# Storing turned attention features by bands of 32 partitions, with the turn two and the store four steps later

## The chip, the cores and the metric

One core of a Trainium2 chip runs the kernel. The metric is the time of one execution on the device in microseconds (us). The engines are named as in the profile: PE is TensorE (matmul) and PEld its weight load, DVE is VectorE, ACT is ScalarE, POOL is GpSimd, and SP (SyncE) issues the DMAs.

## The reference

```python
xn = layernorm(x)                                   # x: 1 x 2048 x 1024
q, k, v = split(xn @ wqkv)                          # 32 heads of 32
pq, pk = q @ w_phi[h], k @ w_phi[h]                 # per head
phi(p) = concat(softmax(p), softmax(-p))            # 64 features a head
num = phi(pq) @ (phi(pk).T @ v)
den = phi(pq) . sum(phi(pk)) + 1e-6
s = (num / den) @ wo
g = silu((sigmoid(xn @ w_gate) * (xn @ w_up)) @ w_down)      # w_gate, w_up: 1024 x 3584
out = x + s * g
```

All of it is in fp32.

## The kernel before, in words

Each large product is done as seven products of blocks in place of eight (B11, B21, T2, T3, T4, T1, B22, in this order), with sums of blocks ahead of and behind them. A number is split into a high and a low part: ACT casts the high part (L137), DVE subtracts it to get the low one (L138), and `mm3` (L146 to L148) makes three matmuls of each pair. PE therefore runs the whole program through, and all else is fitted beside it.

The change lies in the down-projection (`w_down`). It goes through the products, 14 blocks of the inner dimension each, in two halves of four banks; B22 goes through its 14 blocks once for each half. A half of a step is 4 banks x 3 matmuls = 12 matmuls, and then one tick of a counter. `down_load` loads a block of weights (L926) and of activations (L928) into raw buffers (`fa`, `fb`), `down_prep` splits them (L137, L138) into `x` and `w` operands. At the end of a product each bank goes through `evacuate`: behind B21, DVE copies the bank out (L1810), ACT fills it again with the sum kept from B11 (L1811), and the next product, T2, adds to it; behind T1, DVE adds the bank to a kept sum (L1820). `gate_out` applies the gate: ACT (L1794), POOL (L1795), and a store (L1796).

Beside it the query features are finished, in 32 units: 16 tiles of 128 tokens by 2 halves of the heads. Unit n is queued by `q_late` at tick 2 + 24n/5. `later(n, f)` puts a function on the tick n ahead; `tick()` emits what stands on the present tick, behind the latest instruction that was emitted on DVE, ACT and SP. A list scheduler then sets the order of each engine, so ticks order instructions, but nothing on the chip waits for a tick. The steps of a unit are: load of exponentials or raw queries; for raw ones, minimum and maximum (L664, L665), differences (L673, L674), exponentials (ACT, L686) and their sums (L691, L692); `weigh`, a product on POOL in two instructions (L1005); `density`, a row sum and four small ones on DVE (L1010 to L1016); `scale`, a product on POOL in two (L1022); `turn`, a transpose on DVE of 128x1024 by blocks of 32 by 32 (L1026) into one of four slots (`etr`, slots 20 to 23); and `keep`, four stores from that slot to `et_d` in DRAM (L1030).

Behind the last unit, during product B22, the first attention work starts. It loads turned features (L1057), casts them on ACT (L1070) and subtracts on DVE (L1072). The first output of L1070 is slot 20, which was one of the four slots of turned features: it waits for the last turn and for the last stores. In the instruction order below, `x_3_9793` is the block with the four slots of turned features, and `x_4_15940` is what L1070 writes, in the same memory.

The DMAs of SP take turns on eight completion counters (DMAHW0 to DMAHW7 in the order): a DMA is issued only once the one eight places ahead of it has landed. SP issues in order, so a DMA that waits holds up all behind it.

The functions that the diff touches, and what calls them:

Of the kernel before, what the change touches and what calls it, by code (L numbers as in the profile page):

```python
# [19 lines left out]
S, D, H, DH, F = 2048, 1024, 32, 32, 3584  # L20
# [14 lines left out]
class Ring:  # L35
# [3 lines left out]
    def next(self):  # L39
        self.n += 1  # L40
        return self.items[(self.n - 1) % len(self.items)]
# [9 lines left out]
def hedgehog_glu_kernel(  # L51
# [12 lines left out]
    nc = tc.nc  # L64
# [16 lines left out]
    et_d = dram.tile([TT, 2, P, 2 * HB], F32, name="et_d")  # L81
# [39 lines left out]
    def whole(i):  # L121
        return slots[i].rearrange("p a n -> p (a n)")
# [33 lines left out]
    def later(n, f, *a):  # L156
        assert n > 0
        plan.setdefault(clock[0] + n, []).append((f, a))
# [500 lines left out]
    def extremes(name, p):  # L659

        nh = HB // DH
        st = small.tile([P, 4, nh], F32, name=f"st{name}", tag="st", bufs=2)
        pv = p.rearrange("p (h d) -> p h d", d=DH)
        nc.vector.tensor_reduce(st[:, 0], pv, axis=AX.X, op=ALU.max)  # L664
        nc.vector.tensor_reduce(st[:, 1], pv, axis=AX.X, op=ALU.min)  # L665
        return st

    def spread_q(st, p, e):

        pv, mx, mn = [a.rearrange("p (k b d) -> p k b d", b=2, d=d) for a, d in ((p, DH), (st[:, 0], 1), (st[:, 1], 1))]  # L670
        mx, mn = [a.to_broadcast([P, 8, 2, DH]) for a in (mx, mn)]
        ev = e.rearrange("p (b t k d) -> p t k b d", b=2, t=2, d=DH)
        nc.vector.tensor_tensor(ev[:, 0], pv, mx, op=ALU.subtract)  # L673
        nc.vector.tensor_tensor(ev[:, 1], mn, pv, op=ALU.subtract)  # L674
# [10 lines left out]
    def exponentials(e):  # L685
        nc.scalar.activation(e, e, AF.Exp)  # L686

    def inverses(st, e):

        s2, r2 = [st[:, a:a + 2].rearrange("p t h -> p (t h)") for a in (2, 0)]  # L690
        nc.vector.tensor_reduce(s2, e.rearrange("p (g d) -> p g d", d=DH), axis=AX.X, op=ALU.add)  # L691
        nc.vector.reciprocal(r2, s2)  # L692
        return r2
# [284 lines left out]
    def q_late(at, t, hb):  # L978

        hold = {}  # L980

        def load():
            if t < QA:
                hold["e"] = whole(eqr.next())
                nc.sync.dma_start(hold["e"], e_d[t, hb])
                hold["r"] = small.tile([P, 32], F32, name=f"r{t}{hb}", tag="r", bufs=2)
                nc.sync.dma_start(hold["r"], r_d[t, hb])
            else:
                hold["p"] = qraw.next()
                nc.sync.dma_start(hold["p"], qkv_d[Q, t, hb])  # L990

        def first():
            hold["st"] = extremes(f"q{t}{hb}", hold["p"])

        def second():
            hold["e"] = whole(eqr.next())
            spread_q(hold["st"], hold["p"], hold["e"])

        def sums():
            hold["r"] = inverses(hold["st"], hold["e"])  # L1000

        def weigh():
            for a in range(2):
                cols = slice(a * HB, (a + 1) * HB)
                nc.gpsimd.tensor_mul(whole(52)[:, cols], hold["e"][:, cols], zb[hb][:, cols])  # L1005

        def density():
            st = hold["sa"] = small.tile([P, 5, 16], F32, name=f"sa{t}{hb}", tag="sa", bufs=2)
            r, d2, r2 = hold["r"], *[st[:, a:a + 2].rearrange("p t h -> p (t h)") for a in (0, 2)]
            nc.vector.tensor_reduce(d2, whole(52).rearrange("p (g d) -> p g d", d=DH), axis=AX.X, op=ALU.add)  # L1010
            nc.vector.tensor_mul(d2, d2, r)
            r, d2, r2 = [a.rearrange("p (b t k) -> p b t k", b=2, t=2) for a in (r, d2, r2)]
            den = st[:, 4].rearrange("p (b k) -> p b k", b=2)
            nc.vector.scalar_tensor_tensor(den, d2[:, :, 0], EPS_DEN, d2[:, :, 1], op0=ALU.add, op1=ALU.add)
            nc.vector.reciprocal(den, den)
            nc.vector.tensor_mul(r2, r, den[:, :, None].to_broadcast([P, 2, 2, 8]))  # L1016

        def scale():
            e3, r2 = hold["e"].rearrange("p (g d) -> p g d", d=DH), hold["sa"][:, 2:4].rearrange("p t h -> p (t h)")
            for a in range(2):  # L1020
                gs = slice(16 * a, 16 * a + 16)
                nc.gpsimd.tensor_mul(e3[:, gs], e3[:, gs], r2[:, gs, None].to_broadcast([P, 16, DH]))  # L1022

        def turn():
            hold["et"] = whole(etr.next())
            nc.vector.transpose(hold["et"], hold["e"])  # L1026

        def keep():
            for c in range(4):
                nc.sync.dma_start(et_d[t, hb, c * DH:(c + 1) * DH].rearrange("f (a x) -> a f x", a=4),  # L1030
                                  hold["et"][:, c * 256:(c + 1) * 256])

        heavy = ((5, first), (6, second), (9, lambda: exponentials(hold["e"])), (11, sums))
        steps = ((0, load),) + heavy if t >= QA else ((6, load),)
        for n, f in steps + ((11, weigh), (14, density), (15, scale), (18, turn), (18, keep)):
            later(at + n, f)


# [157 lines left out]
    scale = {}  # L1196
# [154 lines left out]
    with in_order(*[getattr(mybir.EngineType, e) for e in ("PE", "DVE", "Activation", "SP", "Pool")]):  # L1351
        for name in FIRST:
            f, found = next((f, m) for form, f in forms for m in [re.fullmatch(form, name)] if m)
# [283 lines left out]
    for n, (kind, c, what, i) in enumerate(ops):  # L1637
# [48 lines left out]
        phase, f = c, what  # L1686
# [144 lines left out]
    for n in range(2 * TT):  # L1831
        q_late(2 + n * 24 // 5, *(light if (n + 1) * QA // TT > n * QA // TT else heavy).popleft())
# [225 lines left out]
```

## Time and profile before

| what | value |
|---|---|
| median of 3 runs | 2350.68 us (2350.02 to 2358.0) |
| time of the profiled execution | 2348.29 us |
| its span (first to last instruction) | 2346.5 us |
| mean granted PE clock | 0.943 of full speed |
| busy: PE, DVE, ACT, POOL | 2307.9, 1750.8, 1231.1, 1153.2 us |
| turns (L1026), 32 | 1634.2 to 2049.6 us |
| stores of turned features (L1030), 128 | 1635.4 to 2054.0 us |
| first attention cast (L1070) | 2062.05 us |

A row of the page or of a view names line, engine, operation and tiles (`out<-in`), how many there were, and the idle time of the engine ahead of them with what ended it. In a timeline the first two numbers are start and length in us, and the bracket holds that idle time.

### The profile page before, as it was taken

The numbers are of one execution on the slowest core, as the hardware profiler recorded it, in microseconds if no ns is written. First come the engines' busy times: TensorE is split into PE (matmuls) and PEld (weight loads), VectorE is DVE, ScalarE is ACT, GpSimd is POOL, SyncE is SP. The second block draws the span as 40 slices with busy tenths as digits, with TensorE's granted clock in tenths as the row PEclk, the third lists the DMA queues.
The fourth block names the chain that finished last, engine by engine and source line by source line (L and its number), as shares of the span: only waits on it lengthen the run. The fifth ranks groups of instructions, "written<-read, shape, count | busy, mean of one in ns | idle before, by whom it ended". The sixth has DMA issues, their size and how long they took to land.

```text
span 2346.5 us, 32121 instructions
## 1 busy us (share of the span) xinstructions
PE 2307.9 (98%) x10533; PEld 1918.4 (82%) x10533; DVE 1750.8 (75%) x2107; ACT 1231.1 (52%) x1965; POOL 1153.2 (49%) x813
## 2 busy tenths in 40 slices
PE   9999999999999999999999999999989999998988
PEld 8888888888888888888888888888878888877777
DVE  8625777876888774777874665657999999977887
ACT  7354577776555555555555545444444345354543
POOL 1323436772231054665653666764464445424676
PEclk9999999999999999999999999999989999989989
DMA  8789977988778868897886867679767666786665
GB/s 298 267 308 364 333 288 286 354 305 311 273 263 296 274 241 281 302 310 265 286 309 222 293 216 246 224 274 352 255 227 241 232 208 217 268 278 218 197 202 178
DMA packets 344185, 631.33 MB, mean 269 GB/s; under 512 B 37841, under 2 KB 87249, under 8 KB 339409
## 3 DMA queue, kind: packets, MB, share of 16 engines
q1 hardware_dynamic: 344016, 629.28, 77.8%
q8 instruction: 82, 1.34, 0.2%
q14 instruction: 87, 0.70, 0.1%
HBM read 378.34 MB, written 250.81 MB: 268 GB/s over the span
## 4 chain that ended last, share of the span: by engine, by line
PE 85%; DVE 6%; DMA 5%; issue 2%; SPq 1%; ACT 1%; POOL 1%; DVEq 0%; ACTq 0%; POOLq 0%
PE bank L147 27%; PE bank L148 27%; PE bank L146 27%; DMA fc<-g_d 2%; PE bank L381 1%; PE bank L744 1%; DMA fa<-h_d 1%; DVE x L1072 1%; DVE x L1107 1%; DVE fb L1072 1%; DMA et_d<-x 1%; DVE w L138 1%; DMA fa<-w_down 0%; DVE x L138 0%; DMA fc<-et_d 0%
## 5 line engine op out<-in xcount | busy, mean ns | idle before, releaser
L146 PE MATMUL bank<-x,w 128*128 128x512 f32 x2248 | 875.1, 390 | 9.9 <-ACT bank L1811 7.5
L147 PE MATMUL bank<-x,w 128*128 128x512 f32 x2248 | 876.7, 390 | 4.9 <-DVE x L138 4.9
L148 PE MATMUL bank<-x,w 128*128 128x512 f32 x2248 | 875.6, 390 | 0.0
L138 DVE TENSOR_TENSOR w<-fa,w 128x512 fp32r<-128x512 f32 (+2 forms) x394 | 395.0, 1009 | 259.0 <-ACT w L137 246.8
L146 PEld LDWEIGHTS bank<-x,w 128*128 128x128 f32 x2248 | 423.1, 188 | 98.7 <-ACT bank L1811 7.9
L147 PEld LDWEIGHTS bank<-x,w 128*128 128x128 f32 x2248 | 423.2, 188 | 93.0 <-DVE x L138 6.1
L148 PEld LDWEIGHTS bank<-x,w 128*128 128x128 f32 x2248 | 422.9, 188 | 87.9
L137 ACT CAST w<-fa 128x512 fp32r<-128x512 f32 (+2 forms) x394 | 267.9, 684 | 318.9 <-PE bank L147 201.4
L146 PE MATMUL bank<-w,x 128*128 128x512 f32 x708 | 278.3, 393 | 0.0
L148 PE MATMUL bank<-w,x 128*128 128x512 f32 x708 | 276.5, 391 | 0.0
L147 PE MATMUL bank<-w,x 128*128 128x512 f32 x708 | 276.4, 390 | 0.0
L148 PEld LDWEIGHTS bank<-w,x 128*128 128x128 f32 x708 | 133.4, 188 | 28.5 <-DVE x L1256 0.7
L146 PEld LDWEIGHTS bank<-w,x 128*128 128x128 f32 x708 | 133.6, 189 | 26.3
L147 PEld LDWEIGHTS bank<-w,x 128*128 128x128 f32 x708 | 133.7, 189 | 26.2
L138 DVE TENSOR_TENSOR w<-fb,w 128x512 fp32r<-128x512 f32 (+1 forms) x116 | 113.8, 983 | 40.3 <-ACT w L137 40.1
L137 ACT CAST w<-fb 128x512 fp32r<-128x512 f32 (+1 forms) x116 | 70.4, 607 | 108.5 <-PE bank L147 80.8
L138 DVE TENSOR_TENSOR x<-fb,x 128x512 fp32r<-128x512 f32 (+1 forms) x87 | 88.7, 1022 | 19.0 <-ACT x L137 16.0
L1401 ACT COPY fc<-bank 128x512 f32<-128x512 f32 x116 | 66.7, 583 | 39.0 <-PE bank L148 15.6
L138 DVE TENSOR_TENSOR p<-fc,p 128x512 fp32r<-128x512 f32 (+1 forms) x68 | 54.6, 813 | 38.4 <-ACT p L137 38.1
L137 ACT CAST x<-fb 128x512 fp32r<-128x512 f32 (+1 forms) x87 | 65.3, 753 | 12.2 <-DMA fb<-xr_d 5.5
L686 ACT ACTIVATE fc<-fc 128x1024 f32<-128x1024 f32 x44 | 46.6, 1060 | 45.2 <-DVE fc L683 27.5
L1096 POOL TENSOR_TENSOR fc<-fc 128x512 f32<-128x512 f32 x32 | 50.0, 1564 | 40.9 <-DVE fc L1091 15.1
(411 smaller groups left out, 3815.0 us busy)
## 6 DMA issues: line engine op xcount, KB each, us to landing
m_d<-fc SPq DMA_DIRECT2D x168, 256.0 KB
fa<-h_d SPq DMA_DIRECT2D x152, 256.0 KB
fa<-wf_d SPq DMA_DIRECT2D x32, 1024.0 KB
x<-m_d SPq DMA_DIRECT2D x128, 256.0 KB
fa<-w_gu SPq DMA_DIRECT2D x102, 256.0 KB
h_d<-fc SPq DMA_DIRECT2D x102, 256.0 KB
fc<-qkv_d SPq DMA_DIRECT2D x86, 256.0 KB
fb<-w_gu SPq DMA_DIRECT2D x72, 256.0 KB
```

What stands on the lines that cost most here:

```text
L137: nc.scalar.copy(o[0], src)
L138: i = nc.vector.tensor_sub(o[1], src, o[0].bitcast(F32))
L146: nc.tensor.matmul(o, a[0], b[0], start=first, stop=False, **kw)
L147: nc.tensor.matmul(o, a[0], b[1], start=False, stop=False, **kw)
L148: last_mm[:] = [nc.tensor.matmul(o, a[1], b[0], start=False, stop=last, **kw).ins]
L381: nc.tensor.matmul(ps[:, gs], r[:, gs], bd[:, 4 * f + g], start=g == 0, stop=g == 3, skip_group_check=True)
L686: nc.scalar.activation(e, e, AF.Exp)
L744: nc.tensor.matmul(kvb[g // 2][:, g % 2 * 256:g % 2 * 256 + 256], v[:, g].rearrange("p a f -> p (a f)"), ph[:, g].rearrange("p a f -> p (a ...
L1072: nc.vector.tensor_sub(lo, src, hi.bitcast(F32))
L1096: nc.gpsimd.tensor_sub(o, a, b)
L1107: nc.vector.tensor_sub(lo, b, hi.bitcast(F32))
L1401: nc.scalar.copy(o, banks[b])
```

## The change

The four stores of a unit each took 256 columns of all 128 partitions. Now each takes one band of 32 partitions with all 1024 columns, in the same pieces of 256 elements. What lies in DRAM afterwards is the same. The turn is put 20 ticks behind the unit's start instead of 18, and the stores 22 instead of 18.

```diff
         def keep():
-            for c in range(4):
-                nc.sync.dma_start(et_d[t, hb, c * DH:(c + 1) * DH].rearrange("f (a x) -> a f x", a=4),
-                                  hold["et"][:, c * 256:(c + 1) * 256])
+            dst = et_d[t, hb].rearrange("(c f) (a x) -> a f c x", c=4, a=4)
+            for a in range(4):
+                nc.sync.dma_start(dst[a], hold["et"][a * DH:(a + 1) * DH].rearrange("f (c x) -> f c x", c=4))
...
-        for n, f in steps + ((11, weigh), (14, density), (15, scale), (18, turn), (18, keep)):
+        for n, f in steps + ((11, weigh), (14, density), (15, scale), (20, turn), (22, keep)):
             later(at + n, f)
```

The instructions are as many as before; their order moves. DVE in the rows that lead to the end of product B21, about 1728 to 1738 us of the profile before (`sa`: the small numbers of `density`; `stq`: those of the raw queries; L1810: the first copies of banks). Before:

```order
L138 TENSOR_TENSOR w_95<-fa_98,w_95 128x512
L692 RECIPROCAL stq_12946<-stq_12946 128x32
L138 TENSOR_TENSOR w_95<-fa_98,w_95 128x512
L1026 STREAM_TRANSPOSE x_3_9793<-x_6_12000 128x1024
L138 TENSOR_TENSOR x_2_5913<-fa_98,x_2_5913 128x512
L138 TENSOR_TENSOR w_95<-fa_98,w_95 128x512
L138 TENSOR_TENSOR w_95<-fb_0_99,w_95 128x512
L1010 TENSOR_REDUCE sa_13143<-fc_101 128x32
L1810 COPY fc_101<-bank_102 128x512
L1810 COPY fc_101<-bank_103 128x512
```

Now:

```order
L138 TENSOR_TENSOR w_95<-fa_98,w_95 128x512
L138 TENSOR_TENSOR w_95<-fb_0_99,w_95 128x512
L1010 TENSOR_REDUCE sa_13138<-fc_101 128x32
L1810 COPY fc_101<-bank_102 128x512
L1810 COPY fc_101<-bank_103 128x512
L138 TENSOR_TENSOR x_2_5913<-fb_0_99,x_2_5913 128x512
L1810 COPY fc_101<-bank_104 128x512
L1011 TENSOR_TENSOR sa_13138<-sa_13138,stq_12941 128x32
L1810 COPY fc_101<-bank_105 128x512
L1026 STREAM_TRANSPOSE x_3_9793<-x_6_12000 128x1024
```

The turn that stood ahead of the first L1810 stands behind the fourth. The turn of the unit ahead of it (at 1718.24 in the profile before) moves in the same way, from ahead of the next unit's L1010 to behind its L1016. DVE before, at that turn:

```order
L138 TENSOR_TENSOR w_95<-fa_98,w_95 128x512
L1026 STREAM_TRANSPOSE x_3_9793<-x_6_12000 128x1024
L1010 TENSOR_REDUCE sa_13029<-fc_101 128x32
L138 TENSOR_TENSOR x_2_5913<-fb_100,x_2_5913 128x512
L138 TENSOR_TENSOR w_95<-fa_98,w_95 128x512
L1011 TENSOR_TENSOR sa_13029<-sa_13029,r_12859 128x32
```

and now:

```order
L1010 TENSOR_REDUCE sa_13024<-fc_101 128x32
L138 TENSOR_TENSOR x_2_5913<-fb_100,x_2_5913 128x512
L1011 TENSOR_TENSOR sa_13024<-sa_13024,r_12855 128x32
L138 TENSOR_TENSOR w_95<-fa_98,w_95 128x512
L1014 SCALAR_TENSOR_TENSOR sa_13024<-sa_13024 128x16
L1015 RECIPROCAL sa_13024<-sa_13024 128x16
L1016 TENSOR_TENSOR sa_13024<-r_12855,sa_13024 128x32
L138 TENSOR_TENSOR w_95<-fa_98,w_95 128x512
L1026 STREAM_TRANSPOSE x_3_9793<-x_6_12000 128x1024
```

The turn moved behind the small numbers of the next unit. ACT where the first attention cast stands among the casts of product B22 (about 2052 to 2066 us of the profile before). Before:

```order
L137 CAST w_95<-fa_98 128x512
L137 CAST x_2_5913<-fa_98 128x512
L1070 CAST x_4_15940<-fc_101 128x1024
L137 CAST w_95<-fa_98 128x512
L1794 ACTIVATE fc_101<-x_5_11999 128x512
```

Now, from the same two casts on:

```order
L137 CAST w_95<-fa_98 128x512
L137 CAST x_2_5913<-fa_98 128x512
L137 CAST w_95<-fa_98 128x512
L1794 ACTIVATE fc_101<-x_5_11999 128x512
L137 CAST x_2_5913<-fa_98 128x512
L137 CAST w_95<-fa_98 128x512
L1794 ACTIVATE fb_100<-x_5_11999 128x512
L137 CAST x_2_5913<-fa_98 128x512
L137 CAST w_95<-fa_98 128x512
L1794 ACTIVATE p_2_9712<-x_5_11999 128x512
L137 CAST x_2_5913<-fb_0_99 128x512
L1070 CAST x_4_15940<-fc_101 128x1024
```

L1070 moved behind six casts, those of three half steps, and three gates. SP's queue at the last unit's stores, before:

```order
L1030 DMA et_d<-x_3_9793 4x32x256 [waits DMAHW4_49,DVE_49]
L926 DMA fb_0_99<-w_down 128x512 [waits DMAHW5_49,DVE_49]
L1030 DMA et_d<-x_3_9793 4x32x256 [waits DMAHW6_49]
L1030 DMA et_d<-x_3_9793 4x32x256 [waits DMAHW7_49]
L1030 DMA et_d<-x_3_9793 4x32x256 [waits DMAHW0_49]
```

Now:

```order
L1031 DMA et_d<-x_3_9793 32x4x256 [waits DMAHW2_49,DVE_49]
L926 DMA fb_100<-w_down 128x512 [waits DMAHW3_49,DVE_49]
L928 DMA fa_98<-h_d 128x512 [waits DMAHW4_49,DVE_49]
L1031 DMA et_d<-x_3_9793 32x4x256 [waits DMAHW5_49]
L926 DMA fa_98<-w_down 128x512 [waits DMAHW6_49,DVE_49]
L928 DMA fa_98<-h_d 128x512 [waits DMAHW7_49,DVE_49]
L1031 DMA et_d<-x_3_9793 32x4x256 [waits DMAHW0_49]
L926 DMA fa_98<-w_down 128x512 [waits DMAHW1_49,DVE_49]
L1031 DMA et_d<-x_3_9793 32x4x256 [waits DMAHW2_49]
```

The four stores now stand spread among the loads of three down steps, and the last of them stands behind an L926 that waits for DVE.

## The prediction

> **What bounds the kernel now.** I read the page's busy times and slices first, then what TensorE (PE) waits for, then its timeline at the two places where it waits inside the stage that the change touches, and last VectorE (DVE), ScalarE (ACT) and SyncE (SP) around these places. The page, engines and two rows of slices:
>
> ```profile
> PE 2307.9 (98%) x10533; PEld 1918.4 (82%) x10533; DVE 1750.8 (75%) x2107; ACT 1231.1 (52%) x1965; POOL 1153.2 (49%) x813
> ...
> PE   9999999999999999999999999999989999998988
> ...
> PEclk9999999999999999999999999999989999989989
> ```
>
> PE is busy for 98%, so only its gaps can be won: 2346.5 - 2307.9 = 38.6 us of the span. The turned features are made between 1634 and 2054 us, slices 28 to 36. Slice 30 falls off in both rows, slice 36 in the clock. What PE waits for, in total, times and longest:
>
> ```profile
> PE bank L146 <- ACT bank L1811: 7.5, 1, 7.5
> PE bank L147 <- DVE x L138: 4.9, 3, 2.5
> ...
> PE bank L146 <- ACT x L137: 2.4, 1, 2.4
> ```
>
> The first gap, PE's timeline (start, length, in brackets the idle time before it):
>
> ```profile
> 1728.41 0.39 PE L148 MATMUL bank<-x,w 128*128 128x512 f32 x1
> 1736.27 0.79 PE L146 MATMUL bank<-x,w 128*128 128x512 f32 x1 [7.47 <-ACT bank L1811]
> ...
> 1740.70 0.41 PE L147 MATMUL bank<-x,w 128*128 128x512 f32 x1
> ```
>
> and the second:
>
> ```profile
> 2061.91 0.39 PE L148 MATMUL bank<-x,w 128*128 128x512 f32 x1
> 2064.71 0.59 PE L146 MATMUL bank<-x,w 128*128 128x512 f32 x1 [2.41 <-ACT x L137]
> 2067.78 0.80 PE L147 MATMUL bank<-x,w 128*128 128x512 f32 x1 [2.48 <-DVE x L138]
> ...
> 2071.79 0.40 PE L147 MATMUL bank<-x,w 128*128 128x512 f32 x1
> ```
>
> The stretches beside them (busy and count of each engine, then granted clock, DMA share, GB/s):
>
> ```profile
> 1700.00:1728.00 28.00, 28.00 (x126) 23.17 (x125) 24.59 (x30) 8.53 (x14) 17.86 (x12) 0.95 0.69 219
> 1736.20:1743.10 6.90, 6.83 (x21) 5.46 (x22) 6.90 (x11) 6.07 (x11) 3.98 (x4) 0.66 0.60 211
> 2067.70:2074.60 6.90, 6.82 (x22) 5.50 (x23) 6.90 (x9) 2.78 (x6) 2.82 (x2) 0.68 0.86 258
> ```
>
> At full rate a matmul takes 28.00/126 = 0.222 us; between the rows of the timeline it is 0.227, which I use, since a row can be missing from the longer count or two fall together. A down step of one half, 12 matmuls, is a tick of 2.72 us. After each gap the granted clock is 0.66 and 0.68 instead of 0.95. From 1728.41 to 1740.70 PE issued 11 matmuls, 2.49 us of work in 12.29: 9.80 us lost (7.47 idle, 2.33 by the clock). From 2061.91 to 2071.79 again 11, in 9.88: 7.39 lost (4.89 idle, 2.50 by the clock). These 17.2 us are all that the change can reach; the other waits lie behind 2120 us, in attention, after the last turn and store.
>
> [...]
>
> **Why PE waits at 1728.** A bank of product B21 is copied by DVE (L1810), then refilled by ACT (L1811), and PE adds on it. DVE and ACT:
>
> ```profile
> 1718.24 1.25 DVE L1026 STREAM_TRANSPOSE x<-x 128x1024 f32<-128x1024 f32 x1 [3.21 <-POOL x L1022]
> ...
> 1730.86 1.23 DVE L1026 STREAM_TRANSPOSE x<-x 128x1024 f32<-128x1024 f32 x1
> 1732.01 0.65 DVE L138 TENSOR_TENSOR x<-fa,x 128x512 fp32r<-128x512 f32 x1
> ...
> 1733.78 1.21 DVE L1010 TENSOR_REDUCE sa<-fc 128x32 f32<-128x1024 f32 x1
> 1734.91 1.28 DVE L1810 COPY fc<-bank 128x512 f32<-128x512 f32 x2
> ```
>
> ```profile
> 1735.63 1.19 ACT L1811 COPY bank<-x 128x512 f32<-128x512 f32 x2 [3.92 <-DVE fc L1810]
> ```
>
> DVE is simply late. All that it waited for from 1672 to 1735 us:
>
> ```profile
> DVE x L1026 <- POOL x L1022: 6.4, 2, 3.2
> DVE x L1026 <- POOL fc L1022: 2.0, 1, 2.0
> ```
>
> 8.4 us, every one in front of a turn (L1026), for the scaling on GpSimd (POOL) just ahead of it.
>
> **Why PE waits at 2062.** The first attention cast writes a slot that the last turned unit still occupies until its stores have landed:
>
> ```profile
> 2062.05 1.04 ACT L1070 CAST x<-fc 128x1024 fp32r<-128x1024 f32 x1 [9.45 <-DMA fb<-w_down]
> ```
>
> ```profile
> 2054.31 0.68 DVE L138 TENSOR_TENSOR x<-fa,x 128x512 fp32r<-128x512 f32 x1
> 2063.13 1.23 DVE L1072 TENSOR_TENSOR x<-fc,x 128x1024 fp32r<-128x1024 f32 x1 [8.14 <-ACT x L1070]
> ```
>
> ```profile
> 2052.70 1.85 SPq L1030 DMA_DIRECT2D et_d<-x  x3
> ...
> 2060.70 0.33 SPq L926 DMA_DIRECT2D fa<-w_down  x1
> ```
>
> The profile names a load as releaser, but that load has no part in L1070; its inputs from the last unit do. The last store was issued by 2054.55 and L1070 started 7.5 us later. ACT and DVE stood in front of L1070 and L1072, the casts and subtractions (L137, L138) of the next down steps behind them, and PE ran dry.
>
> **The change part by part.** *Turn two ticks later.* The 32 turns keep their work (1.23 us each on DVE) but each stands behind the sums of the next unit. POOL's scaling pair then has two ticks more, 5.4 us, against a longest wait of 3.2; I take the 8.4 us as gone. In the new order one turn, 1.15 us of DVE (1730.86 to 1732.01), also moves from ahead of the first L1810 to behind the fourth. L1810 comes to 1734.91 - 8.4 - 1.15 = 1725.4, L1811 0.72 later, 1726.1, its end 0.6 later, 1726.7. PE wants the bank at 1728.41 + 0.23 = 1728.6: 1.9 us to spare, the gap goes, -9.80.
>
> What takes the wait's place: L1010, the row sum, now reaches its input (POOL's L1005) earlier, because no turn stands ahead of it. POOL's rows:
>
> ```profile
> 1720.76 3.27 POOL L1005 TENSOR_TENSOR fc<-fc,x 128x512 f32<-128x512 f32 x2 [2.55 <-DVE sa L1010]
> 1724.88 2.45 POOL L1022 TENSOR_TENSOR x<-x,sa 128x512 f32<-128x512 f32 x2 [0.85 <-DVE sa L1016]
> ```
>
> The L1010 ahead of the first L1810 needs the pair that ended at 1724.03, and would itself stand at 1733.78 - 9.55 = 1724.2. Even if POOL came no earlier it would not wait; POOL itself waited 2.55 us there for DVE, so it comes earlier. The far bound is that only the last wait counts, 3.21 + 1.15 = 4.4: then L1811 ends at 1731.8, 3.2 us of gap and up to 2.33 of slow clock stay, and the gain is 4.3 instead of 9.8.
>
> *Store four ticks later.* Before, SP met a store whose turn was not done and everything behind it waited; two ticks between turn and store end that. In these rows of SP's queue (1640 to 2040 us) the first kind is a load waiting for a store eight DMAs earlier to land:
>
> ```profile
> SPq L1030 <- DVE x L1026: 24.5, 17, 5.7
> SPq L928 <- DMA et_d<-x: 23.7, 23, 2.2
> ```
>
> None of these reached PE between 1743 and 2061, where it had no gap, so both are costed at nothing; the raw blocks loaded ahead cover them, and without that cover 2.2 us, the longest, is what one would cost. The loads (L926, L928) that now pass ahead of a store go out sooner, never later.
>
> For the end of the stage the shift counts against itself: the last four stores go out later, L1070 as well. In ACT's order L1070 stands behind three more down steps' casts, so PE is fed 3 x 2.72 = 8.2 us longer, to 2062.1 + 8.2 = 2070.3. From L1070 to PE's restart it took 2067.78 - 2062.05 = 5.7, so L1070 must start by 2064.6. The last store stands behind an L926 that waits for the subtraction that ended at 2055.0; before, the load in that place of the queue left at 2060.7. Between these ends I take the middle, 2057.8, because most of the loads ahead of it were themselves held by stores. With the same 7.5 us to land, L1070 starts at 2065.3: 0.7 us late (bounds 2.1 early and 3.6 late). I charge 0.7 and, as a shorter gap than either, 1.8 of slow clock instead of 2.5: 2.5 us stay of the 7.39; bounds 0 and the whole.
>
> *Bands of 32 partitions.* Four stores of 128 KB a unit as before, in pieces of 256 elements as before; the 128 issues cost SP the same 0.5 us each:
>
> ```profile
> L1030 SPq DMA_DIRECT2D et_d<-x x128: 503/514/1444, 1635.4 to 2054.0; - x128
> ```
>
> What may change is the time to land. The chain of waits has two stores and a load of twice the size:
>
> ```profile
> 2004.93 5.12 DMA et_d<-x
> 2026.76 8.54 DMA et_d<-x
> 2035.36 6.77 DMA fa<-h_d
> ```
>
> A band store may land like the quicker one, 2.4 us under the 7.5 that I used, and the 2.5 us vanish; or 2 to 4 us later, and they grow to the 7.39. I take 7.5 unchanged, near the middle of the rows.
>
> [...]
>
> **The sum.** 2348.29 for the profiled execution - 9.80 - 7.39 + 2.5 = 2333.6. The execution's time is 2.39 under the median of the runs, so 2336.0.
>
> **Rivals.**
> Only the first gap goes: the last stores land late or the loads behind them do, and L1070 stops the casts as long as before. For it speaks that the stores move by 10.9 us of ticks and L1070 by 8.2 only; against it that DVE's and SP's waits ahead of them shrink. 2350.68 - 9.8 = 2340.9.
>
> Only the second goes: L1810 stays late, since DVE, ahead of time, next waits for ACT's casts, which wait for PE to leave a buffer. Against it the 1.9 us to spare. With the far bound of 4.3: 2350.68 - 7.39 + 2.5 - 0 to 4.3 is 2341.5 to 2345.8.
>
> Nothing moves: waits change names, turn for row sum, and stores land as late: 2349 to 2352. For it: DVE was idle in front of a turn because POOL was late, and POOL has as much to do as before. Against it: two ticks are more than any of these waits.
>
> Slower: band stores land so late that the queue of SP starves the loads. Only eight DMAs are in flight, and all the way from 1640 to 2040 us went
>
> ```profile
> q1 hardware_dynamic: 59318, 93.53, 71.0%
> ...
> et_d<-x SPq DMA_DIRECT2D x116, 128.0 KB
> ```
>
> 116 stores, 15.2 MB, and 78.3 MB more, some 299 transfers of 256 KB: 415 in 400 us. Eight in flight allow a mean of 8 x 400/415 = 7.7 us to land. With 6.5 for the others (72%), stores decide from (7.7 - 0.72 x 6.5)/0.28 = 10.8 us on; each us beyond is 0.28/7.7 = 3.6% of 400 us, 14.5 us. At 11.8 us: about 2365 us. Against it: 8.54 is the longest that the chain shows.
> [...]
>
> **How the numbers follow.** Both gaps all or mostly gone: 0.50, with 2331 to 2340 as its own range; only the first 0.22; only the second 0.08; nothing moves 0.12; slower 0.08. A change under 0.5% (11.8 us) can hardly be told from none here. 2336.0 is 0.6% faster; the first case alone passes 2338.9, all but a little, which the chance that the first rival comes out better makes up: faster 0.50. The next three are within 0.5%: 0.42. Slower 0.08. The range, 2330 to 2354, leaves out the slower rival and some 0.04 below.
>
> **What would show it.** In the changed kernel's profile: no wait of L1026 for L1022; L1810 near 1725 and no PE idle time at 1728, granted clock 0.95 throughout; L1070 near 2065, its idle time under 6 us, and PE idle for at most a few us before 2075; PE's idle sum near 27 instead of 38.6. Wrong would be: L1010 waiting over 2 us for L1005 in front of L1810; L1070 idle over 9 us; a load waiting over 3 us for a store to land, many times; or a gap at another change of product, such as L1820 near 2040, where a turn stands ahead of the bank sums in both orders.

## The result and the profile after

The changed kernel takes 2335.77 us (median of 5 runs, 2332.84 to 2337.9), the one before 2350.68 (2346.59 to 2358.0). The ratio is 0.9932, interval 0.9912 to 0.9952: faster by 0.7%. The profiled execution took 2334.47 us with a span of 2332.7, 13.8 less than before. One execution of a kernel below (bands at 18 and 22) took 2551.78 us at a granted clock of 0.85 and is left out of its median.

The page of the changed kernel, the rows that answer to those of before:

```profile
PE 2300.2 (99%) x10533; PEld 1913.7 (82%) x10533; DVE 1737.7 (74%) x2107; ACT 1231.7 (53%) x1965; POOL 1150.0 (49%) x813
...
PE   9999999999999999999999999999999999998888
...
PEclk9999999999999999999999999999999999999999
```

The two hollows, slices 30 and 36, are gone; only the end, where the change alters no instruction, is below 9. What PE waits for in the whole run:

```profile
PE bank L1082 <- DVE x L1072: 14.7, 5, 3.2
PE bank L1082 <- DVE fb L1072: 4.3, 7, 0.8
PE bank L146 <- DMA x<-wo_d: 2.9, 3, 1.9
PE bank L147 <- DVE x L138: 2.9, 3, 1.6
```

The 7.5 us for L1811 and the 2.4 for L137 no longer stand there. PE in the stretches of the two gaps (busy and count, then clock, DMA share, GB/s):

```profile
1736.20:1743.10 6.90, 6.90 (x32) 5.74 (x31) 6.90 (x10) 5.47 (x12) 6.77 (x5) 1.00 0.99 320
2030.00:2060.00 30.00, 30.00 (x134) 24.87 (x133) 27.05 (x32) 18.13 (x32) 11.83 (x8) 1.00 0.81 268
2060.00:2075.00 15.00, 15.00 (x68) 12.44 (x67) 11.08 (x17) 9.27 (x17) 3.76 (x3) 1.00 0.87 307
```

32 matmuls stand where 21 stood, at the full clock, and there is no gap from 2030 to 2075. PE at the first gap, from the last L148 ahead of it:

```profile
1727.31 0.39 PE L148 MATMUL bank<-x,w 128*128 128x512 f32 x1
1727.54 0.39 PE L146 MATMUL bank<-x,w 128*128 128x512 f32 x1
```

That L148 started at 1728.41 in the kernel before: this execution was 1.1 us ahead when it came to the stage's first gap. DVE's and ACT's timelines at the end of product B21:

```profile
1716.32 1.23 DVE L1026 STREAM_TRANSPOSE x<-x 128x1024 f32<-128x1024 f32 x1
...
1724.78 1.21 DVE L1010 TENSOR_REDUCE sa<-fc 128x32 f32<-128x1024 f32 x1
1725.91 1.27 DVE L1810 COPY fc<-bank 128x512 f32<-128x512 f32 x2
...
1729.70 1.23 DVE L1026 STREAM_TRANSPOSE x<-x 128x1024 f32<-128x1024 f32 x1
```

```profile
1726.61 1.19 ACT L1811 COPY bank<-x 128x512 f32<-128x512 f32 x2 [1.16 <-DVE fc L1810]
```

No bracket stands behind a turn: none of the 32 waited for POOL. L1810 starts 9.0 us earlier, 7.9 of it against the last L148. All that DVE waited for from 1672 to 1735 us:

```profile
DVE w L138 <- ACT w L137: 1.0, 3, 0.6
```

At the second place, ACT's and SP's timelines, and the view of the stores by line:

```profile
2053.93 1.05 ACT L1070 CAST x<-fc 128x1024 fp32r<-128x1024 f32 x1 [3.28 <-DMA fa<-w_down]
```

```profile
2048.74 0.47 SPq L1031 DMA_DIRECT2D et_d<-x  x1
```

```profile
L1031 SPq DMA_DIRECT2D et_d<-x x128: 303/430/1313, 1641.4 to 2048.7; - x128
...
DMA to landing us min/median/max: 2.0/2.9/5.9
```

L1070 started 4.7 us after the last store's issue ended (7.5 before), stood for 3.3 us instead of 9.45, and PE did not notice.

Three marks split the gain: the first L1820 (end of T1) came at 2040.8 before and at 2030.3 now, 10.5 us earlier; the first L1823 (end of B22's first half) at 2087.1 and 2069.3, 17.8 earlier; the end 13.8 earlier. Of this, 1.1 us stood ahead of both gaps, so the stage itself won 16.7. And 4.0 us were lost again at the end; the last experiments look at that.

### The profile page after: what moved, and what is told of

Same layout as the page of the kernel before. It is cut to its first block, busy times and chain, and to the rows that moved or that the text cites. A ratio compares the mean times of both kernels' runs of the same rounds, so it can differ in the third digit from the quotient of the medians.

```text
span 2332.7 us, 32121 instructions
## 1 busy us (share of the span) xinstructions
PE 2300.2 (99%) x10533; PEld 1913.7 (82%) x10533; DVE 1737.7 (74%) x2107; ACT 1231.7 (53%) x1965; POOL 1150.0 (49%) x813
## 4 chain that ended last, share of the span: by engine, by line
PE 88%; DVE 5%; DMA 4%; issue 1%; POOL 1%; SPq 1%; ACT 1%; DVEq 0%; ACTq 0%; POOLq 0%
PE bank L147 28%; PE bank L146 28%; PE bank L148 28%; DMA fc<-g_d 1%; PE bank L381 1%; PE bank L744 1%; DVE x L1072 1%; DVE x L1107 1%; DMA x<-w_phi 1%; DVE fb L1072 1%; DVE w L138 0%; DMA x<-x 0%; DVE fa L1107 0%; SPq L1057 0%; POOL fc L1096 0%
## 5 line engine op out<-in xcount | busy, mean ns | idle before, releaser
L147 PE MATMUL bank<-x,w 128*128 128x512 f32 x2248 | 876.3, 390 | 2.9 <-DVE x L138 2.9
L148 PE MATMUL bank<-x,w 128*128 128x512 f32 x2248 | 874.7, 390 | 0.0
L138 DVE TENSOR_TENSOR w<-fa,w 128x512 fp32r<-128x512 f32 (+2 forms) x394 | 392.2, 1000 | 259.2 <-ACT w L137 252.0
L147 PEld LDWEIGHTS bank<-x,w 128*128 128x128 f32 x2248 | 422.4, 188 | 90.5 <-DVE x L138 4.2
L148 PEld LDWEIGHTS bank<-x,w 128*128 128x128 f32 x2248 | 422.3, 188 | 87.2
L137 ACT CAST w<-fa 128x512 fp32r<-128x512 f32 (+2 forms) x394 | 268.2, 684 | 328.9 <-PE bank L147 196.4
L148 PE MATMUL bank<-w,x 128*128 128x512 f32 x708 | 276.8, 391 | 0.0
L147 PE MATMUL bank<-w,x 128*128 128x512 f32 x708 | 276.7, 391 | 0.0
L148 PEld LDWEIGHTS bank<-w,x 128*128 128x128 f32 x708 | 133.3, 188 | 28.3 <-DVE x L1256 0.7
L147 PEld LDWEIGHTS bank<-w,x 128*128 128x128 f32 x708 | 133.5, 188 | 26.1
L138 DVE TENSOR_TENSOR w<-fb,w 128x512 fp32r<-128x512 f32 (+1 forms) x116 | 109.6, 947 | 45.1 <-ACT w L137 42.3
L137 ACT CAST w<-fb 128x512 fp32r<-128x512 f32 (+1 forms) x116 | 70.3, 607 | 103.7 <-PE bank L147 79.0
L138 DVE TENSOR_TENSOR x<-fb,x 128x512 fp32r<-128x512 f32 (+1 forms) x87 | 85.0, 979 | 22.8 <-ACT x L137 22.5
L138 DVE TENSOR_TENSOR p<-fc,p 128x512 fp32r<-128x512 f32 (+1 forms) x68 | 54.2, 808 | 43.7 <-ACT p L137 40.8
L137 ACT CAST x<-fb 128x512 fp32r<-128x512 f32 (+1 forms) x87 | 65.3, 753 | 13.1 <-DMA fb<-xr_d 6.2
```

The lines of the kernel that those rows point to most:

```text
L137: nc.scalar.copy(o[0], src)
L138: i = nc.vector.tensor_sub(o[1], src, o[0].bitcast(F32))
L147: nc.tensor.matmul(o, a[0], b[1], start=False, stop=False, **kw)
L148: last_mm[:] = [nc.tensor.matmul(o, a[1], b[0], start=False, stop=last, **kw).ins]
```

## The experiments

Theory A, the prediction's own: the first gap belongs to the turn's place on DVE, the second to when the last stores have landed. Theory B: the old stores crowd the DMA and make both. Theory C: the ticks do all. "Bands" and "quarters" name the shape of a store, and the two numbers are the ticks of turn and store. Every edit is to the changed kernel or to the kernel before, in `q_late` alone; of the line with the ticks only the part that changes is shown. Each ratio is to executions of the kernel before in the same round, whose median was 2351.31 us for the first four, 2351.02 for bands at 19 and 19 and 2352.04 for the other three.

**Bands at 18 and 18.**

```diff
-(15, scale), (20, turn), (22, keep)
+(15, scale), (18, turn), (18, keep)
```

> Stores by bands, turn and store at their old ticks (18, 18). Theory A (the first gap belongs to the turn's place on DVE, the second to how long the last stores take to land): L1026 still waits about 8 us for L1022 between 1672 and 1735 us, PE still waits 7 to 8 us for L1811; the last stores land in 3 to 5 us instead of 7.5, L1070 starts near 2058 and the second gap shrinks from 4.9 us idle to 0 to 1.5; time 5 to 7.4 us under before, near 2344. Theory B (old stores crowd the DMA and make both gaps): both gaps gone, 14 to 15 us under before. Theory C (the ticks do all): both gaps as before, no change.

2343.35 us, ratio 0.9971 (0.9961 to 0.9980). Its waits of PE, of DVE from 1672 to 1735 us, and its L1070:

```profile
PE bank L146 <- ACT bank L1811: 6.9, 1, 6.9
```

```profile
DVE x L1026 <- POOL x L1022: 6.4, 2, 4.5
DVE x L1026 <- POOL fc L1022: 2.0, 1, 2.0
```

```profile
2054.72 1.05 ACT L1070 CAST x<-fc 128x1024 fp32r<-128x1024 f32 x1 [4.99 <-DMA fb<-w_down]
```

The first gap stays with the 8.4 us of waits that the kernel before had; the second is gone, with L1070 two casts earlier in ACT's order than before. Theories B and C fall: bands alone take the second gap and leave the first.

**Quarters at 20 and 22.**

```diff
-(15, scale), (18, turn), (18, keep)
+(15, scale), (20, turn), (22, keep)
```

> Stores by quarters of the columns as before, turn and store at the new ticks (20, 22). Theory A: the first gap is gone (9.8 us), the last stores take 5 to 8.5 us to land and L1070 starts near 2055 to 2058 in the shorter program (before's 2065 to 2068), so 0 to 5 us of the second gap stay; 10 to 15 us under before, 2336 to 2341. Theory B: both gaps stay, no change. Theory C: both gaps gone, 14 to 15 us under before, L1070 as early as in the changed kernel.

2347.81 us, ratio 0.9988 (0.9978 to 0.9998), far less than A or C gave. Its waits of PE, DVE's from 1672 to 1735 us, and L1070:

```profile
PE bank L146 <- ACT x L137: 7.4, 1, 7.4
PE bank L147 <- DVE x L138: 4.6, 5, 1.6
```

```profile
DVE sa L1010 <- POOL fc L1005: 2.4, 1, 2.4
```

```profile
2067.14 1.04 ACT L1070 CAST x<-fc 128x1024 fp32r<-128x1024 f32 x1 [11.33 <-DMA et_d<-x]
```

It is not B's picture either: no wait for L1811 is left, so the turn's place does take the first gap without bands. But the second gap grew. From the first L1820 to the first L1823 it took 50.5 us, the kernel before 46.3, the changed one 39.0: the second gap cost 11.5 us instead of 7.3. Old stores issued later are a loss of 4.2 us, nearly half of the first gain. The row sum L1010 also waited for POOL here, as one rival said, and the first L1810 came 0.8 us ahead of the last L148 (1727.62 and 1728.44), with bands 1.4 us ahead.

**Bands at 20 and 20.**

```diff
-(20, turn), (22, keep)
+(20, turn), (20, keep)
```

> Stores by bands, turn at tick 20, store on the same tick instead of two later. Theory A: first gap gone by the turn; L1070 stands one half step earlier in ACT's order than in the changed kernel but its stores go out as much earlier and land in 3 to 5 us: both gaps gone, 13 to 15 us under before, as the changed kernel within 2 us. Rival: the two ticks between turn and store matter, because SP meets a store whose turn is not done and holds the loads behind it (25 us of such waits before): then PE waits for loads and the time is 3 us or more above the changed kernel.

2335.66 us, ratio 0.9934 (0.9920 to 0.9948). Both gaps are gone, L1070 started at 2048.91 and had waited 1.60 us. The two ticks between turn and store are worth nothing that can be measured.

**Bands at 18 and 22.**

```diff
-(20, turn), (22, keep)
+(18, turn), (22, keep)
```

> Stores by bands, turn at its old tick 18, store at tick 22. Theory A: the first gap stays (the turn still waits about 8 us for L1022 and stands ahead of L1810), the second is gone or under 1.5 us: 5 to 7.4 us under before, near 2344, as with bands at 18 and 18. Theory B: both gone, 14 to 15 us under before.

2345.93 us, ratio 0.9976 (0.9968 to 0.9985). The first gap stays (7.3 us idle at L1811). L1070 starts at 2061.96 after waiting 6.99; from L1820 to L1823 it took 43.1 us, 4.1 over the changed kernel. Later stores cost something with bands too when L1070 does not move along (here it stands two ACT rows later, in the changed kernel nine): more than theory A's 1.5.

**Quarters at 20 and 20.**

```diff
-(15, scale), (18, turn), (18, keep)
+(15, scale), (20, turn), (20, keep)
```

> Stores by quarters of the columns, turn at tick 20 and store on the same tick. Theory A: the first gap is gone by the turn's place as in the kernel with quarters at 20 and 22; L1070 stands one half step earlier in ACT's order and the last old stores go out one to two half steps earlier, so the second gap is between that of the kernel before (4.9 us idle) and that of quarters at 20 and 22 (8.6 us idle): about 2343, 6 to 9 us under before. Rival (the first gap goes only with bands, because old stores delay the loads that POOL waits for): the first gap stays and the time is no lower than before by more than 3 us.

2346.67 us, ratio 0.9972 (0.9961 to 0.9983): 5.4 us under before (2352.04 in this round), short of the 6 to 9. The first gap shrank to 1.1 us idle (L1810 at 1729.4), the second grew to 7.5 (L1820 to L1823 in 49.6). So the order is theory A's, with two sizes off: old stores also make POOL and DVE a little late at the first gap (L1010 waited 3.6 us for L1005, with bands at these ticks not at all), and cost more at the second when issued later.

**Bands at 19 and 19.**

```diff
-(20, turn), (22, keep)
+(19, turn), (19, keep)
```

> Stores by bands, turn and store at tick 19. In DVE's order the turns near 1718 and 1731 us still stand ahead of the next L1010, and one still ahead of the first L1810. Theory A (the first gap hangs on the order of turn and next unit on DVE, which only tick 20 changes): L1026 waits 4 to 8 us for L1022 between 1672 and 1735 us, the first gap stays with 5 to 7.5 us idle, the second is gone by the bands; 5 to 8 us under before, as with bands at 18 and 18. Rival (any delay of the turn frees POOL in proportion): one tick is 2.7 of the 3.2 us of the longest wait, so the waits shrink to about 1 us, the first gap goes, and the time is that of the changed kernel, 14 to 15 us under before.

2340.58 us, ratio 0.9954 (0.9940 to 0.9968), 10.4 us under before and between the two theories. DVE's waits from 1672 to 1740, and PE's:

```profile
DVE x L1026 <- POOL x L1022: 5.7, 1, 5.7
```

```profile
PE bank L146 <- ACT bank L1811: 4.3, 1, 4.3
```

One tick takes some of the wait and about 3 us of the gap (4.3 idle, where 6.9 to 7.5 stood). Tick 20, where the turn passes the next unit's L1010 to L1016, takes the rest.

**Eight and sixteen stores a unit.** These ask why bands land sooner: theory D below looks at the slowest dimension of a store's DRAM side, 4 before (4x32x256) and 32 with bands (32x4x256), theory E at its bytes or its partitions. Eighths, with 2:

```diff
-            dst = et_d[t, hb].rearrange("(c f) (a x) -> a f c x", c=4, a=4)
-            for a in range(4):
-                nc.sync.dma_start(dst[a], hold["et"][a * DH:(a + 1) * DH].rearrange("f (c x) -> f c x", c=4))
+            dst = et_d[t, hb].rearrange("(c f) (g a x) -> c g a f x", c=4, g=2, a=2)
+            for c in range(4):
+                for g in range(2):
+                    nc.sync.dma_start(dst[c, g], hold["et"][g * 64:(g + 1) * 64, c * 256:(c + 1) * 256])
```

> Eight stores a unit, each of 64 partitions by 256 columns (DRAM side 2x32x256), at ticks 20 and 22; the same bytes in the same pieces of 1 KB. Theory D (the number of DMA engines that a store gets goes by its slowest dimension: 2 here, 4 before, 16 with bands): while only these stores are in flight the DMA share falls to about 0.13 and 49 GB/s; 512 KB a unit take 10.7 us on two engines, 13.1 us between units, and every load has a share on them, so PE waits for loads again and again: slower than before by 20 us or more. Theory E (the landing time goes by the bytes of a store or by how many partitions it has): 64 KB stores land as fast as bands, 2 to 4 us, and the time is within 5 us of the changed kernel.

Sixteenths, in place of the same three lines:

```diff
+            dst = et_d[t, hb].rearrange("(c f) (a x) -> c a f x", c=4, a=4)
+            for c in range(4):
+                for a in range(4):
+                    nc.sync.dma_start(dst[c, a], hold["et"][a * DH:(a + 1) * DH, c * 256:(c + 1) * 256])
```

> Sixteen stores a unit, each of 32 partitions by 256 columns (DRAM side 32x256), at ticks 20 and 22; the same bytes in the same pieces of 1 KB, twice as many DMAs as with eighths. Theory D: all 16 DMA engines carry them, no stretch at a quarter or an eighth of the DMA share; only SP has more to issue (16 x 0.4 us = 6.4 us a unit, 12 more stores in the eight lanes): 0 to 10 us over the changed kernel and far below the eighths. Theory F (the number of DMAs decides): slower than the eighths.

Eighths take 2480.28 us (ratio 1.0543), sixteenths 2381.42 (1.0122), two runs each. Stretches of 1 us in which hardly anything but stores was in flight (the last two numbers are DMA share and GB/s), the kernel before:

```profile
2055.00:2056.00 1.00, 1.00 (x6) 0.83 (x5) 0.00 (x0) 0.00 (x0) 0.00 (x0) 0.95 0.27 96
2056.00:2057.00 1.00, 1.00 (x6) 0.82 (x5) 0.00 (x0) 0.00 (x0) 0.00 (x0) 0.95 0.27 98
```

eighths:

```profile
1744.00:1745.00 1.00, 0.00 (x0) 0.00 (x0) 1.00 (x3) 0.93 (x2) 0.00 (x0) 0.50 0.13 48
```

and the changed kernel while it moved nothing but the four bands of one unit (issued from 1819.44 on), early and late:

```profile
1820.25:1821.25 1.00, 1.00 (x6) 0.84 (x5) 1.00 (x4) 0.93 (x2) 0.00 (x0) 1.00 0.91 197
1821.75:1822.00 0.25, 0.25 (x3) 0.21 (x2) 0.25 (x2) 0.00 (x0) 0.00 (x0) 1.00 1.03 361
```

The DMA share was 0.27 with a slowest dimension of 4, 0.13 with 2, and 0.92 with 32 (from 1820.25 to 1822.00, at 220 GB/s): in these three kernels the share goes with this dimension, as theory D had it, and theory E falls, since eighths are smaller than bands and slower (48 GB/s against 220). Sixteenths, twice as many DMAs as eighths, are 99 us faster than these. But they are 46 us slower than bands, where theory D gave 0 to 10. The price of a DMA more was too low: their stores land in 1.9 us (median), yet the 512 stores queue in the eight lanes of SP (37 of them waited 14.7 us for one kind of load alone, `fa<-h_d`, between 1640 and 2040 us), the loads stand behind them, and PE idles 26.9 us from 1640 to 2120 (2.9 in the changed kernel), in waits for casts and sums. By SP's rows from 1640 to 2040 us, added up, it spent 301 of the 400 us issuing (176 in the changed kernel) and 57 waiting for earlier DMAs to land (20), so the 0.4 us of each issue seem to weigh more than the lanes; no run separates the two.

**The end.** The changed kernel and the one before were run once more for a second profile.

> The changed kernel once more, for a second profile of its end. If the 3 to 4 us that it lost behind 2200 us (PE idle 15.2 us there, 11.6 before, in waits for L1072 of 2.7 to 3.2 us each) belong to the order, the sum is again 14 to 17 us; if they come from one execution's DMA, it may be anything from 10 to 17.

> The kernel before once more, for a second profile: both gaps again, 7 to 8 us at L1811 and 4 to 6 us behind L1070; PE idle behind 2200 us 9 to 17 us if that end differs from one execution to the next, near 11.6 if it belongs to the order; the granted clock in stretches without a gap either 0.95 again or 1.00.

2333.22 and 2351.57 us. PE's idle time behind 2200 us, added up from its timeline: 9.5 us in the second profile of the changed kernel against 15.2 in the first; 17.6 in the second of the kernel before against 11.6. In the six others with all stores in 128 KB it is 10.5 to 16.9. So, as far as these profiles show, the 4 us belong to the execution and not to the change. The waits are alike in all, in the changed kernel's DVE timeline:

```profile
2187.06 0.69 DVE L1946 TENSOR_TENSOR fc<-fc,bank 128x512 f32<-128x512 f32 x1 [3.43 <-DMA fc<-g_d]
2187.66 1.22 DVE L1072 TENSOR_TENSOR x<-fc,x 128x1024 fp32r<-128x1024 f32 x1
```

A product waits for a gate's load, and the subtraction that PE wants stands behind it. By these rows, how long the load takes sets the wait; no run varied it.

All of it in one table (first starts in us; "second" is the first L1820 to the first L1823). Starts count from the start of the span; the executions already differ ahead of the gaps, the last L148 before the first one starting at 1726.6 (bands 20, 20) to 1731.1 us (bands 19, 19), so the two columns of lengths compare better than the two of starts.

| kernel | median | idle at L1811 | L1820 | second | L1070 |
|---|---|---|---|---|---|
| before | 2350.68 | 7.5 | 2040.8 | 46.3 | 2062.1 |
| before, again | 2351.57 | 7.4 | 2042.9 | 46.2 | 2064.1 |
| bands 18, 18 | 2343.35 | 6.9 | 2040.4 | 39.5 | 2054.7 |
| bands 18, 22 | 2345.93 | 7.3 | 2040.9 | 43.1 | 2062.0 |
| bands 19, 19 | 2340.58 | 4.3 | 2038.5 | 40.2 | 2055.4 |
| quarters 20, 20 | 2346.67 | 1.1 | 2033.7 | 49.6 | 2063.2 |
| quarters 20, 22 | 2347.81 | none | 2033.2 | 50.5 | 2067.1 |
| bands 20, 20 | 2335.66 | none | 2029.7 | 39.0 | 2048.9 |
| changed (bands 20, 22) | 2335.77 | none | 2030.3 | 39.0 | 2053.9 |
| changed, again | 2333.22 | none | 2032.5 | 39.0 | 2055.8 |

## Why the prediction was right, and where it was not

*What can be won.* 17.2 us in two gaps. Between the same matmuls, from the last L148 ahead of the first gap to the eleventh behind it, PE took 12.29 us before and takes 2.49 now: the 9.80 of the forecast. The 7.39 of the second gap went whole. Behind both the changed kernel is 17.8 us ahead, less the 1.1 from ahead of the stage and 0.5 that it lost near 1978 (L147 waited 0.21 us for L138). In the second pair, whose L148 start together, it is 17.6. This step was right, and the table shows that the two gaps could be taken one by one.

*The first gap: right, but by less than was put.* L1810 was put at 1725.4 and came at 1725.9, which is 1727.0 in the time of the kernel before (1.1 added): 7.9 us earlier, not 9.55. L1811 ended at 1727.2, and PE took the bank at 1727.54: 0.3 us to spare (0.4 in the second profile), not 1.9. The 8.4 us of waits went, and L1010 did not take them over, but DVE filled part of the time with other work (27.69 of the 28 us from 1700 to 1728 busy, 24.59 before). So the whole gap went by a narrow margin. Bands at 18 and 18 show that the turn's place was the cause. What the step lacked: with quarters L1810 starts 0.8 us ahead of the last L148 (20, 22) or 0.1 behind it (20, 20), with a wait of L1010 for L1005, where bands give 1.4 and 1.1 ahead. Part of the spare time came from bands, which the step had costed at nothing there.

*The second gap: the term that was mis-sized.* The prediction kept 2.5 us of it, because it took the 7.5 us to land unchanged. Bands land in 2.0 to 5.9 us, 2.9 in the middle, the last one in 5.0, and nothing was kept. The last store left at 2048.74, which is 2059.2 in the time of the kernel before (10.5 added), later than the middle of 2057.8 but inside its ends; L1070 came at 2064.4 in that time, against 2065.3 put and 2064.6 needed. So two misses met here: the store left 1.4 us later than put, and its shorter landing made up for more than that. Without the 2.5 the same sum gives 2333.5. How little of the DMA the old stores kept busy could have been seen: the rows of 2055 to 2057 above, with 0.27 of the DMA share, were in the trace of before. That is about what four busy engines of sixteen would give, but no view shows single engines.

*The later store.* The prediction counted L1070's later place as a gain and the later store as a loss of about the same size. With quarters the two together cost 4.2 us (50.5 against 46.3). With bands they cost nothing, and without the later ticks (18, 18) the second gap is gone as well. Of the change's three parts, bands took the second gap, the turn's tick the first, and the store's tick nothing.

*SP's waits.* Two ticks between turn and store were to end SP's waits for a turn. They did not: in the changed kernel from 1640 to 2040 us

```profile
SPq L1031 <- DVE x L1026: 22.2, 19, 3.3
```

stands where 24.5 stood. What went are the loads' waits for a store to land, 23.7 and 4.6 us. As forecast, neither reached PE.

*The end.* It was taken as untouched. It gave 4.0 us back in the first pair of profiles, within what it differs from one execution to the next. In this pair 14.7 us were forecast; the stage won 16.7, 1.1 stood ahead of it, and 4.0 went at the end: 13.8. That 2336.0 came as close as it did to the median (2335.77) is luck: the interval of the ratio, 11.3 to 20.7 us, cannot tell 14.7 from the 17.2 of both gaps.

*The rivals.* "Only the first gap goes" is what quarters at 20 and 22 would have been, and worse: the second gap grows. "Slower" had the wrong shape for bands, but the right one for eighths: from 1640 to 2040 us 180 GB/s moved (235 before), PE waited 36.2 us for L138 in the whole run (4.9 before), and the kernel lost 128 us (against 2352.04).

*Few partitions in a band.* By the order of issue the first two bands, partitions 0 to 63, come first in the rows at 1820 us: 197 GB/s at 0.91 of the DMA share, twice the 96 to 98 that the old stores had. Behind them, when bands of the other half should run as well, the three quarters of a us from 1821.25 to 1822.00 show 147, 246 and 361 GB/s at 0.85, 0.95 and 1.03, together 251 at 0.94. Whether its few partitions cost a band anything is not shown: which bands moved when is read from the order of issue alone, and no run tests it.

## What to carry to other kernels

Where a DMA's access pattern begins with a small dimension, try reordering it so that a larger one comes first (here 32 in place of 4, with 0.92 of the DMA share in place of 0.27), even if each transfer then covers fewer partitions: here the same bytes in as many stores of the same pieces landed in 2.9 us (median) and stopped holding up the loads (L926 and L928: 28.3 us of such waits before, from 1640 to 2040 us, and no such row after). But don't pay for it with more DMAs: sixteen in place of four cost 46 us. And before a store is issued later, look for who waits for its buffer at the end of the stage: that wait hit ACT, and through the casts queued behind it PE, only at the last of 32 units.

## What the runs showed that was not expected

A short gap cost more than its idle time. In bands at 18 and 22, PE idled 1.42 and 0.84 us near 2064, and seven of the matmuls just behind started 0.43 us apart instead of 0.23; 2.3 us of idle time became 4.1 lost. In the second gap of the kernel before, where the clock was 0.68 behind it, no idle stretch passed 2.48 us, and these were shorter still. What the clock went by here stays open.

The first profile of the kernel before had a granted clock of 0.95 in stretches without a gap, and its second, like all others, 1.00. The matmuls were equally far apart in both (126 and 125 in the 28 us from 1700 to 1728). So here a difference of 5% in this number between two executions went with no difference in speed; within one it shows the gaps.
